# Self-attention block on one core: another set of planner parameters, and the output projection of the third query block in one piece

## The chip, the core and the metric

The kernel runs on one core of one Trainium2 chip. The metric is the device time of one execution in microseconds. A core has five engines that run side by side and wait for each other through semaphores: TensorE (PE in the profile, its weight loads PEld), VectorE (DVE), ScalarE (ACT), GpSimd (POOL) and SyncE (SP, which here only issues transfers).

## The reference

Inputs: x of 1x2048x448, wqkv of 448x1344, wo of 448x448, all in bfloat16. Sixteen heads of width 28.

```python
qkv = transpose((x @ wqkv).reshape(B, S, 3, H, Dh), 2, 0, 3, 1, 4)
scores = einsum("bhqd,bhkd->bhqk", q, k) * (Dh ** -0.5)
p = softmax(scores, axis=-1)
o = einsum("bhqk,bhkd->bhqd", p, v)
return transpose(o, 0, 2, 1, 3).reshape(B, S, D) @ wo
```

The exponentials, 16 x 2048 x 2048 of them, are most of the work that is not a matmul.

## The kernel before

The sixteen heads are four groups g of four heads; the queries are four blocks c of 512. One (g, c) is a window, 16 in all, run g by g. A window has 16 rows of keys (128 keys each) times four heads, so 64 tiles of 128x512 scores, 1024 tiles in all; `WT` is 64 and `NT` 1024.

Per tile, `emit_S` (L656) computes the transposed scores into PSUM. Two engines make exponentials of them:

- ScalarE (L946) takes two tiles at once from a double bank PA_199 or PA_200 and writes a PTA tile of 128x1024.
- VectorE and GpSimd share another tile, from a single bank PD_201, PD_202 or PD_203, in `start_tile` (L744): the first pass on VectorE (L751) scales the low 16 bits of the scores to DU, the second pass on VectorE (L754) multiplies the same low halves from PSUM with DU and makes DV, GpSimd (L757) multiplies DV by DU and makes DG, and the third pass on VectorE (L770) adds DG to the scores and writes the bits of a bfloat16 into a PTD tile. The product is a cubic correction of the exponential's mantissa.

A row of four exponentials then goes through four small matmuls with the values (`pv_op`, L807), which sum into bank PO; a column of ones in the values gives the denominators. At the end of a window `finish_window` copies PO to OSB (L698), sends the denominators through DRAM to all partitions (L723 to L728, issued by SyncE), and GpSimd multiplies (L731) into OT[g][c]. Once all four groups of a block c are there, `task_OP(c)` (L613) multiplies them by wo: four blocks of 128 queries, for each a sum over g of matmuls of 128x448, then a copy by VectorE, then the block's store (L635). Block 3, the last window's, is done by code behind the plan (L1062 on): the last two rows of keys are left over (`NLAST`), `task_pre` (L590) sums three groups of the projection ahead, `partial_sums` copies PO (L688) and gathers the denominators by matmul into PD_203 (L674), and then L1080 to L1102 add the last two rows, normalise, project and store.

The order of every engine's instructions is not written out: a planner in the kernel (L991 on) simulates the engines with assumed durations (`P1`, `PTT`, `MM` and others), picks for each engine the ready task of the lowest priority number, and then emits the instructions in the order found. On the chip each engine runs its list in that order. The parameters that the change touches steer it:

- `O1`, `O2`, `OF`: tile n's first, second and third pass have the priorities n - O1, n - O2 and n - OF.
- `NTAIL`: VectorE takes no tiles within the last NTAIL; from there the single banks are free for the tasks of the end.
- `GLAT`: the time the planner assumes for the broadcast of the denominators (L728).
- `J0`, `J3`, `JL`: how many rows must be ready before a window's first PV; J3 is for the last four windows except the very last, which has JL.
- `SLK`: by how much a task on TensorE may run past the end of an exponential when the next scores are due.
- `DI`: with how many VectorE tiles under way, at least, the projection may be taken early near the end.

With `SPLIT = (2,)` block 2's projection is cut in two: `task_part` (L600) sums groups 0 to 2 (L605) during the last four windows, where PARTD, PARTE and PARTU set its priority, its earliest moment and the point from which it may use any single bank, and VectorE copies the sums in float32 (L608) into the space of a key tile no longer used. `task_OP` then does group 3 alone for that block (L621), and VectorE adds the stored sums (L625) in place of the copy (L628).

Of the kernel before, what the change touches and what calls it, by code (L numbers as in the profile page):

```python
# [10 lines left out]
ALU = mybir.AluOpType  # L11
# [3 lines left out]
F32 = mybir.dt.float32  # L15
# [3 lines left out]
P = 128  # L19
H = 16  # L20
HP = 32
G = 4
# [17 lines left out]
SEM = 0.13  # L40
# [35 lines left out]
def kernel(  # L76
# [7 lines left out]
    nc = tc.nc  # L84
    _, S, D = x.shape
# [4 lines left out]
    TPC = QW // P  # L90
# [13 lines left out]
    PMODE = 'g'  # L104
    PBACK = 3
    J0 = 9
    NTAIL = 12
    JL = 6
    DI = 2
    WPE = 1  # L110
    PVM = 0.0
    ADUR = 0.25
# [6 lines left out]
    PFIN = 0.3  # L119
    QEA = 30  # L120
    PLT = 6.0
    GLAT = 6.5
    J3 = 9
    UQ = 16
    OD = 4
    PADQ = 1
    O1 = 30
    O2 = 10
    OF = 0.4
    RV = 2  # L130
    QPR = 100
    LOOK = 0.2
    SLK = 0.13
    MG = 0.1
    SPLIT = (2,)
    PARTD = 60
    PARTE = -4
    PARTU = 40
    UO = 40

    x2 = x[0]
# [15 lines left out]
    WO = sb([P, G, D], BF16, "WO")  # L157
# [4 lines left out]
    KB = [[sb([P, S], BF16, f"KB{b}_{pr}") for pr in range(2)] for b in range(2)]  # L162
# [4 lines left out]
    OT = [[sb([P, QW], BF16, f"OT{g}_{c}") for c in range(NQC)] for g in range(G)]  # L167
# [11 lines left out]
    OUTS = XS  # L179
# [62 lines left out]
    for i in range(HG):  # L242
        nc.sync.dma_start(out=WO[HP * i:HP * i + Dh, :, :],
                          in_=bass.AP(wo.tensor, wo.offset + i * Dh * D, [[D, Dh], [HG * Dh * D, G], [1, D]]))
# [3 lines left out]
    NT = G * NQC * NKT * HG  # L248
# [8 lines left out]
    def add(op):  # L257
        static[op.eng].append(op)
        return op

    def bank_task():
        return {"slot": None}

    def acq_d(task, early=False, urgent=1e9):
        def f(t):
            if task["slot"] is not None:
                return True
            free = [s for s in ([o_slot] + d_slots if early or pos[0] >= min(urgent, NT - NTAIL) else [o_slot]) if s.free_at <= t + 1e-9]
            if not free:
                return False  # L270
            s = free[-1]
            s.free_at = 1e18
            task["slot"] = s
            return True
        return f
# [4 lines left out]
    def at(n):  # L280
        return lambda t: pos[0] >= n

    def bank(task):
        return (PD + [PO])[task["slot"].idx]
# [76 lines left out]
    WT = NKT * HG  # L361

    def chain_mm(n, fn, deps, prio, elig, acq):
        ops = []
        for k in range(n):
            o = add(Op("PE", MM, (lambda k=k: fn(k)), deps=deps if k == 0 else [ops[-1]], prio=prio + 0.001 * k, kind="B",
                       elig=elig, acq=acq if k == 0 else None, lat=0.0 if k < n - 1 else PLAT))
            ops.append(o)
        return ops
# [205 lines left out]
    ot_done = {}  # L575
# [16 lines left out]
                [ot_done[(g, c)] for g in range(G - 1)], NT + 900 + tq * 10, None, hold(acq, tq))  # L592

    op_left = [TPC * (NQC - 1)]
    parts = {}

    def part(c, tq):
        return KB[0][tq // 2][:].bitcast(F32)[:, (tq % 2) * D:(tq % 2 + 1) * D]

    def task_part(c):  # L600
        due = (12 + c) * WT - PARTD
        for tq in range(TPC):
            task = bank_task()
            ap = (lambda task=task: bank(task)[:, 0:D])
            ops = chain_mm(G - 1, lambda g, tq=tq, ap=ap: nc.tensor.matmul(  # L605
                out=ap(), lhsT=OT[g][c][:, tq * P:(tq + 1) * P], rhs=WO[:, g, :], start=(g == 0), stop=(g == G - 2)),
                [ot_done[(g, c)] for g in range(G - 1)], due + tq * 10, at(12 * WT - PARTE), acq_d(task, urgent=due + PARTU))
            ev = add(Op("DVE", 0.54, lambda tq=tq, ap=ap: nc.vector.tensor_copy(out=part(c, tq), in_=ap()),  # L608
                        deps=[ops[-1]], prio=due - 1000))
            ev.after = lambda t, task=task: setattr(task["slot"], "free_at", t + SEM)  # L610
            parts[(c, tq)] = ev

    def task_OP(c):  # L613
        due = (12 + c + 1) * WT + 16
        st = add(Op("SP", 0.05, None, prio=due))
        evs = []
        for tq in range(TPC):
            task = bank_task()
            ap = (lambda task=task: bank(task)[:, 0:D])
            g0 = G - 1 if c in SPLIT else 0  # L620
            ops = chain_mm(G - g0, lambda k, tq=tq, ap=ap: nc.tensor.matmul(  # L621
                out=ap(), lhsT=OT[g0 + k][c][:, tq * P:(tq + 1) * P], rhs=WO[:, g0 + k, :], start=(k == 0), stop=(g0 + k == G - 1)),
                [ot_done[(g, c)] for g in range(g0, G)], due + tq * 10, None, acq_d(task, urgent=NT - UO))
            if g0:
                ev = add(Op("DVE", 0.56, lambda tq=tq, ap=ap: nc.vector.tensor_tensor(  # L625
                    out=OUTS[c][:, tq, :], in0=ap(), in1=part(c, tq), op=ALU.add), deps=[ops[-1], parts[(c, tq)]], prio=due - 1000))
            else:
                ev = add(Op("DVE", 0.54, lambda tq=tq, ap=ap: nc.vector.tensor_copy(out=OUTS[c][:, tq, :], in_=ap()),  # L628
                            deps=[ops[-1]], prio=due - 1000))
            def aft(t, task=task):  # L630
                op_left[0] -= 1
                task["slot"].free_at = t + SEM
            ev.after = aft
            evs.append(ev)
        add(Op("SP", 0.05, lambda: nc.sync.dma_start(out=out_perm[:, c * TPC:(c + 1) * TPC, :], in_=OUTS[c][:]),  # L635
               deps=evs, prio=due))
# [55 lines left out]
    def finish_window(w, t):  # L692
        g, c = divmod(w, NQC)
        b = norm_n[0] % 2
        norm_n[0] += 1
        pvop = rows[(w, NKT - 1)]["pv"]
        prev = norm_busy[b]
        ev = add(Op("DVE", 0.62, lambda: nc.vector.tensor_copy(out=OSB[b][:], in_=PO[:]), deps=[pvop] + ([prev] if prev else []),  # L698
                    prio=-5000))

        def rel(t):
            o_slot.free_at = t + SEM
        ev.after = rel

        if w >= NW - WPE:
            ev.after = None
            d1 = chain_A(lambda tq: den_gather(PO, lambda k: OSB[b][:, k * P:(k + 1) * P], (tq,)), [ev])
            d2 = add(Op("DVE", 0.17, lambda: nc.vector.reciprocal(out=RT[:], in_=PO[:, 0:TPC * HG]), deps=[d1], prio=-5000))
            d2a = [add(Op("DVE", 0.25, lambda hf=hf: den_expand(hf, nc.vector.tensor_copy), deps=[d2], prio=-5000)) for hf in range(2)]
            d2b = chain_A(lambda tq: den_spread(PO, (tq,)), d2a)  # L710
            d3 = add(Op("DVE", 0.62, lambda: nc.vector.tensor_tensor(out=OT[g][c][:], in0=OSB[b][:], in1=PO[:], op=ALU.mult),
                        deps=[d2b], prio=-5000))
            d3.after = rel
            norm_busy[b] = d3
            ot_done[(g, c)] = d3
            if (g, c) == (G - 2, NQC - 1):
                task_pre()
            if g == G - 2 and c in SPLIT:
                task_part(c)
            if g == G - 1:  # L720
                task_OP(c)
            return
        o1 = [add(Op("SP", 0.6, lambda: nc.sync.dma_start(  # L723
            out=DCO[b][:], in_=OSB[b][Dh::HP, :].rearrange("i (a b) -> i a b", b=TPC * HG)), deps=[ev], prio=-10, lat=2.6))]
        o2 = add(Op("DVE", 0.17, lambda: nc.vector.reciprocal(out=DRC[b][:], in_=DCO[b][:]), deps=o1, prio=-4000))
        o3 = add(Op("SP", 0.4, lambda: nc.sync.dma_start(out=SCR[b][:].rearrange("i (a b) -> (i a) b", b=TPC * HG),
                                                         in_=DRC[b][:]), deps=[o2], prio=-10, lat=2.0))
        o4 = [add(Op("SP", 0.6, lambda: nc.sync.dma_start(  # L728
            out=RRB[b][:], in_=bass.AP(SCR[b][:].tensor, SCR[b][:].offset, [[QW, HG], [0, HP], [1, QW]])),
            deps=[o3], prio=-10, lat=GLAT))]  # L730
        o5 = add(Op("POOL", 1.22, lambda: nc.gpsimd.tensor_tensor(out=OT[g][c][:], in0=OSB[b][:], in1=RRB[b][:], op=ALU.mult),  # L731
                    deps=o4, prio=-10, kind="n"))
        norm_busy[b] = o5
        ot_done[(g, c)] = o5
        if (g, c) == (G - 2, NQC - 1):
            task_pre()
        if g == G - 2 and c in SPLIT:
            task_part(c)
        if g == G - 1:
            task_OP(c)  # L740

# [249 lines left out]
    while True:  # L991
        if not times:
            break
        t = heapq.heappop(times)
# [67 lines left out]
    c = NQC - 1  # L1062
    g = G - 1
# [11 lines left out]
    for j in range(NKT - NLAST, NKT):  # L1075
        pt = rows[(NW - 1, j)]["p"]
        for i in range(HG):
            for tq in range(TPC):
                col = tq * HG + SI[i]
                nc.tensor.matmul(out=PD[2][:, col:col + 1], lhsT=pt[i][1]()[:, tq * P:(tq + 1) * P],  # L1080
                                 rhs=VA[g][:, 0, 0, Dh:Dh + 1], start=False, stop=(j == NKT - 1), skip_group_check=True)
        for i in range(HG):
            st = SI[i]
            nc.tensor.matmul(out=PO[HP * st:HP * (st + 1), :], lhsT=VA[g][:, j, st, :], rhs=pt[i][1](),
                             start=False, stop=(j == NKT - 1), tile_position=(0, HP * st), skip_group_check=True)
# [44 lines left out]
```

## Time and profile before

| what | value |
|---|---|
| three runs | 416.57, 416.38, 416.83 us; median 416.57 |
| profiled execution | 416.57 us, of which the span from first to last instruction is 414.5 |
| busy: TensorE | 364.7 us (88% of the span) |
| busy: VectorE | 396.0 us (96%), 700 instructions |
| busy: ScalarE | 399.6 us (96%), 439 instructions |
| busy: GpSimd | 226.3 us (55%), 211 instructions |
| chain that ended last | ScalarE 85%, issue 7%, TensorE 5% |
| granted TensorE clock | 1.000 |
| transfers | 15.85 MB, 14.4% of 16 engines' span on the main queue |

An engine that waits inside an instruction's queue shows as idle time in front of it, with the releaser's name. ScalarE's and VectorE's instructions overlap a little in the record: a VectorE pass lasts 0.68 us, but follows the one before by 0.60, and the exponential of two tiles is recorded with 0.92 to 1.29 us while they follow each other every 0.917. Where a chain of such instructions is counted, the distance from start to start is the cost. The chain of waits goes back from the last instruction and names what each one waited for.

### The profile page before, as it was taken

Reading aid. Unit: us, or ns where it says so; the run is one execution under the profiler, and the core shown is the slowest. Engines: PE = TensorE matmul, PEld = TensorE weight load, DVE = VectorE, ACT = ScalarE, POOL = GpSimd, SP = SyncE. Lnnn points to the kernel's source line nnn. Section 1 sums busy time; section 2 is a strip of 40 time slices with the busy share of each in tenths; the row PEclk is TensorE's granted clock in tenths of the full one; section 3 lists DMA queues with packets and bytes.
Section 4 is the critical chain, followed back from the end, with each engine's and each line's share of the span. In section 5 each row is a group of like instructions: output and inputs, shape, how many; then the busy total and the mean of one; then the engine's idle time right before and its main releaser. Section 6 shows DMA issues by size and latency. Waiting matters only on the chain.

```text
span 414.5 us, 7646 instructions
## 1 busy us (share of the span) xinstructions
PE 364.7 (88%) x2655; PEld 124.8 (30%) x2668; DVE 396.0 (96%) x700; ACT 399.6 (96%) x439; POOL 226.3 (55%) x211
## 2 busy tenths in 40 slices
PE   8988989898988889898897988889897988989996
PEld 5433222323232232323222222222322222222324
DVE  6899999999999999999999999999999999999983
ACT  4999999999999999999999999999999999999992
POOL 3155456474656656475555646456474656556450
PEclk9999999999999999999999999999999999999999
DMA  8410010202201002111400001010410101001012
GB/s 258 76 19 21 3 49 9 55 22 56 69 2 46 0 22 36 26 32 23 100 3 29 18 19 30 2 41 6 90 35 12 36 1 47 0 27 47 20 53 90
DMA packets 33414, 15.85 MB, mean 38 GB/s; under 512 B 26016, under 2 KB 30304, under 8 KB 33376
## 3 DMA queue, kind: packets, MB, share of 16 engines
q1 hardware_dynamic: 32304, 15.05, 14.4%
q8 instruction: 21, 0.34, 0.3%
q10 hardware_dynamic: 1072, 0.32, 0.3%
q14 instruction: 17, 0.14, 0.1%
HBM read 7.37 MB, written 1.96 MB: 23 GB/s over the span
## 4 chain that ended last, share of the span: by engine, by line
ACT 85%; issue 7%; PE 5%; DMA 1%; DVE 1%; SPq 0%; DVEq 0%
ACT PTA_132 L946 4%; ACT PTA_133 L946 4%; ACT PTA_131 L946 4%; ACT PTA_134 L946 4%; ACT PTA_140 L946 4%; ACT PTA_139 L946 4%; ACT PTA_138 L946 4%; ACT PTA_137 L946 4%; ACT PTA_136 L946 4%; ACT PTA_135 L946 4%; ACT PTA_145 L946 4%; ACT PTA_141 L946 4%; ACT PTA_144 L946 3%; ACT PTA_148 L946 3%; ACT PTA_149 L946 3%
## 5 line engine op out<-in xcount | busy, mean ns | idle before, releaser
L757 POOL TENSOR_TENSOR DG_183<-DV_177,DU_171 128x512 f16<-128x512 f16 x30 | 34.7, 1155 | 36.9 <-DVE DV_177 L754 36.7
L757 POOL TENSOR_TENSOR DG_184<-DV_178,DU_172 128x512 f16<-128x512 f16 x30 | 34.7, 1156 | 30.1 <-DVE DV_178 L754 29.5
L757 POOL TENSOR_TENSOR DG_186<-DV_180,DU_174 128x512 f16<-128x512 f16 x29 | 33.5, 1155 | 30.7 <-DVE DV_180 L754 29.3
L757 POOL TENSOR_TENSOR DG_185<-DV_179,DU_173 128x512 f16<-128x512 f16 x30 | 34.7, 1156 | 23.6 <-DVE DV_179 L754 23.5
L757 POOL TENSOR_TENSOR DG_188<-DV_182,DU_176 128x512 f16<-128x512 f16 x29 | 33.5, 1155 | 24.1 <-DVE DV_182 L754 23.0
L757 POOL TENSOR_TENSOR DG_187<-DV_181,DU_175 128x512 f16<-128x512 f16 x29 | 33.5, 1156 | 23.6 <-DVE DV_181 L754 23.4
L656 PEld LDWEIGHTS <-KB_1_94 64*128 64x128 bf16 x256 | 20.5, 93 | 46.1 <-issue 45.1
L656 PEld LDWEIGHTS <-KB_0_93 64*128 64x128 bf16 x256 | 20.5, 93 | 46.0 <-issue 45.0
L656 PEld LDWEIGHTS <-KB_0_91 64*128 64x128 bf16 x256 | 20.4, 92 | 45.0 <-issue 41.3
L656 PEld LDWEIGHTS <-KB_1_92 64*128 64x128 bf16 x256 | 20.1, 92 | 45.3 <-issue 43.4
L946 ACT ACTIVATE PTA_145<-PA_199 128x1024 bf16<-128x1024 f32 x18 | 22.5, 1253 | 0.0
L946 ACT ACTIVATE PTA_144<-PA_200 128x1024 bf16<-128x1024 f32 x18 | 22.5, 1247 | 0.0
L946 ACT ACTIVATE PTA_140<-PA_200 128x1024 bf16<-128x1024 f32 x18 | 22.4, 1247 | 0.0
L946 ACT ACTIVATE PTA_143<-PA_199 128x1024 bf16<-128x1024 f32 x18 | 22.4, 1244 | 0.0
L946 ACT ACTIVATE PTA_142<-PA_200 128x1024 bf16<-128x1024 f32 x18 | 22.3, 1240 | 0.0
L946 ACT ACTIVATE PTA_141<-PA_199 128x1024 bf16<-128x1024 f32 x18 | 22.3, 1237 | 0.0
L946 ACT ACTIVATE PTA_146<-PA_200 128x1024 bf16<-128x1024 f32 (+1 forms) x18 | 21.9, 1216 | 0.0
L946 ACT ACTIVATE PTA_139<-PA_199 128x1024 bf16<-128x1024 f32 x17 | 21.1, 1242 | 0.0
L946 ACT ACTIVATE PTA_147<-PA_199 128x1024 bf16<-128x1024 f32 x17 | 21.1, 1241 | 0.0
L751 DVE TENSOR_SCALAR DU_173<-PD_203 128x512 f16<-128x512 uint16 x29 | 19.8, 682 | 0.9 <-PE PD_203 L656 0.7
L751 DVE TENSOR_SCALAR DU_171<-PD_201 128x512 f16<-128x512 uint16 x29 | 19.8, 681 | 0.9 <-PE PD_201 L656 0.9
L751 DVE TENSOR_SCALAR DU_174<-PD_201 128x512 f16<-128x512 uint16 x29 | 19.7, 680 | 0.7 <-PE PD_201 L656 0.7
(632 smaller groups left out, 1516.6 us busy)
## 6 DMA issues: line engine op xcount, KB each, us to landing
RRB_195<-SCR_197 SPq DMA_DIRECT2D x8, 256.0 KB
RRB_196<-SCR_198 SPq DMA_DIRECT2D x7, 256.0 KB
KB_1_94<-KB_0_93 SPq DMA_DIRECT2D x4, 128.0 KB
XS_127<-in_x_dram SPq DMA_DIRECT2D x1, 448.0 KB
XS_128<-in_x_dram SPq DMA_DIRECT2D x1, 448.0 KB
XS_129<-in_x_dram SPq DMA_DIRECT2D x1, 448.0 KB
XS_130<-in_x_dram SPq DMA_DIRECT2D x1, 448.0 KB
out_dram<-XS_127 SPq DMA_DIRECT2D x1, 448.0 KB
```

The costliest lines, as they stand in the source:

```text
L656: nc.tensor.matmul(out=ap, lhsT=KB[g % 2][i // 2][a:a + 64, j * P:(j + 1) * P], rhs=QB[w % NQB][i // 2][a:a + 64, :], start=True, stop=Tru ...
L751: p1 = add(Op("DVE", P1, lambda: nc.vector.tensor_scalar(out=DU[b][:], in0=lo, scalar1=SIG / 65536, scalar2=SIG * (SS - 0.5), op0=ALU.mult ...
L757: gq = add(Op("POOL", PTT, lambda: nc.gpsimd.tensor_tensor(out=DG[b][:], in0=DV[b][:], in1=DU[b][:], op=ALU.mult), deps=[p2], prio=n, kind ...
L946: nc.scalar.activation(out=PTA[pslot.idx][:, 0:len(ns) * QW], in_=PA[s.idx][:, 0:len(ns) * QW], func=ACT.Exp, bias=ACT_BIAS, scale=ACT_SCALE)
```

## The change

Described in a few words, the change is: "VectorE's tile: second pass multiplies the scores' low halves from PSUM with the first pass's result, GpSimd makes the cubic's last product for every tile, in place of: VectorE tiles free of the share". The diff has two parts. It sets eight planner parameters to other values, and it takes out SPLIT with all that belongs to it, so that block 2's projection is one sum over four groups, as those of blocks 0 and 1 are. The lines of VectorE's tile (L751 to L773) are the same in both kernels.

```diff
-    NTAIL = 12
+    NTAIL = 6
     JL = 6
-    DI = 2
+    DI = 1
...
-    GLAT = 6.5
-    J3 = 9
+    GLAT = 7.0
+    J3 = 7
     UQ = 16
     OD = 4
     PADQ = 1
-    O1 = 30
-    O2 = 10
-    OF = 0.4
+    O1 = 20
+    O2 = 20
+    OF = 10
     RV = 2
     QPR = 100
     LOOK = 0.2
-    SLK = 0.13
+    SLK = 0.15
     MG = 0.1
-    SPLIT = (2,)
-    PARTD = 60
-    PARTE = -4
-    PARTU = 40
     UO = 40
...
-    parts = {}
-
-    def part(c, tq):
-        return KB[0][tq // 2][:].bitcast(F32)[:, (tq % 2) * D:(tq % 2 + 1) * D]
-
-    def task_part(c):
...
     def task_OP(c):
...
-            g0 = G - 1 if c in SPLIT else 0
-            ops = chain_mm(G - g0, lambda k, tq=tq, ap=ap: nc.tensor.matmul(
-                out=ap(), lhsT=OT[g0 + k][c][:, tq * P:(tq + 1) * P], rhs=WO[:, g0 + k, :], start=(k == 0), stop=(g0 + k == G - 1)),
-                [ot_done[(g, c)] for g in range(g0, G)], due + tq * 10, None, acq_d(task, urgent=NT - UO))
-            if g0:
-                ev = add(Op("DVE", 0.56, lambda tq=tq, ap=ap: nc.vector.tensor_tensor(
-                    out=OUTS[c][:, tq, :], in0=ap(), in1=part(c, tq), op=ALU.add), deps=[ops[-1], parts[(c, tq)]], prio=due - 1000))
-            else:
-                ev = add(Op("DVE", 0.54, lambda tq=tq, ap=ap: nc.vector.tensor_copy(out=OUTS[c][:, tq, :], in_=ap()),
-                            deps=[ops[-1]], prio=due - 1000))
+            ops = chain_mm(G, lambda g, tq=tq, ap=ap: nc.tensor.matmul(
+                out=ap(), lhsT=OT[g][c][:, tq * P:(tq + 1) * P], rhs=WO[:, g, :], start=(g == 0), stop=(g == G - 1)),
+                [ot_done[(g, c)] for g in range(G)], due + tq * 10, None, acq_d(task, urgent=NT - UO))
+            ev = add(Op("DVE", 0.54, lambda tq=tq, ap=ap: nc.vector.tensor_copy(out=OUTS[c][:, tq, :], in_=ap()),
+                        deps=[ops[-1]], prio=due - 1000))
...
-            if g == G - 2 and c in SPLIT:
-                task_part(c)
```

The last two lines are taken out at both places where `finish_window` had them.

More of the change, by code (lines that the diff above doesn't have):

```diff
@@ L594 @@
     op_left = [TPC * (NQC - 1)]
-    parts = {}
-    def part(c, tq):
-        return KB[0][tq // 2][:].bitcast(F32)[:, (tq % 2) * D:(tq % 2 + 1) * D]
-    def task_part(c):
[L601 to L608, printed above, removed]
-                        deps=[ops[-1]], prio=due - 1000))
-            ev.after = lambda t, task=task: setattr(task["slot"], "free_at", t + SEM)
-            parts[(c, tq)] = ev
     def task_OP(c):
@@ L619, in task_OP @@
             ap = (lambda task=task: bank(task)[:, 0:D])
-            g0 = G - 1 if c in SPLIT else 0
-            ops = chain_mm(G - g0, lambda k, tq=tq, ap=ap: nc.tensor.matmul(
-                out=ap(), lhsT=OT[g0 + k][c][:, tq * P:(tq + 1) * P], rhs=WO[:, g0 + k, :], start=(k == 0), stop=(g0 + k == G - 1)),
-                [ot_done[(g, c)] for g in range(g0, G)], due + tq * 10, None, acq_d(task, urgent=NT - UO))
-            if g0:
-                ev = add(Op("DVE", 0.56, lambda tq=tq, ap=ap: nc.vector.tensor_tensor(
-                    out=OUTS[c][:, tq, :], in0=ap(), in1=part(c, tq), op=ALU.add), deps=[ops[-1], parts[(c, tq)]], prio=due - 1000))
-            else:
-                ev = add(Op("DVE", 0.54, lambda tq=tq, ap=ap: nc.vector.tensor_copy(out=OUTS[c][:, tq, :], in_=ap()),
-                            deps=[ops[-1]], prio=due - 1000))
+            ops = chain_mm(G, lambda g, tq=tq, ap=ap: nc.tensor.matmul(
[3 more added lines that the diff above has]
+                        deps=[ops[-1]], prio=due - 1000))
             def aft(t, task=task):
@@ L736, in finish_window @@
             task_pre()
-        if g == G - 2 and c in SPLIT:
-            task_part(c)
         if g == G - 1:
```

## The prediction

> **What bounds the kernel now.** I read the page's busy shares, then the table by stage, then the chain that ended last, then the timeline of the last 14 us. ScalarE (96%) and VectorE (96%) tie on the page, so the stages decide. Two rows of that table (columns: stretch, length, busy us of PE, PEld, DVE, ACT, POOL, clock, DMA share, GB/s):
>
> ```profile
> 20.00:400.00 380.00, 336.32 (x2417) 109.17 (x2428) 373.94 (x644) 380.00 (x416) 220.14 (x191) 1.00 0.12 30
> 404.46:414.60 10.14, 6.19 (x71) 4.17 (x69) 3.74 (x9) 1.96 (x4) 0.00 (x0) 1.00 0.26 92
> ```
>
> From 20 to 400 us ScalarE has no idle time at all (380.00 of 380.00), VectorE has 6 us, TensorE 44. The exponentials end one after another: the first ends at 16.19 + 1.02 = 17.21, the last whole one (two tiles) at 403.17 + 1.29 = 404.46, so 422 steps take 387.25 us, 0.918 each; the undisturbed run at 18.47 to 36.80 us has 0.917. At most 422 x 0.001 = 0.5 us is lost in the whole stretch. After 404.46 ScalarE has nothing to do, and the chain goes over to TensorE:
>
> ```profile
> 403.61 0.35 PE PA_200 L656
> 403.96 0.30 PE PD_203 L621
> 404.26 0.57 PE PD_201 L590 x3
> 404.83 0.38 PE PD_202 L590 x2
> 405.21 0.82 PE PD_203 L674 x8
> 406.03 0.21 PE PD_202 L590
> 406.24 0.38 PE PD_203 L1080 x16
> ```
>
> So the end is a sum: 424 passes of ScalarE, then what TensorE has queued behind the last score matmul (403.59), in its fixed order. Between that matmul and the first L1080 (406.08 in the timeline) lie one output projection matmul, six of the last block's, and the gather of the denominators. From 406.08 on (last two rows of keys, normalisation, last projection, stores) 8.4 us of span follow, the same instructions in both kernels.
>
> **The change, part by part.**
>
> The words promise a new form of VectorE's tile. The diff has no line of it: the second pass on low halves (L754) and GpSimd's product (L757, 177 tiles) already stand in the kernel before. That part costs nothing.
>
> The exponentials. The built order gives ScalarE 424 passes in both kernels; before, the last one holds one tile, now two (847 and 848 tiles; VectorE's tiles fall from 177 to 176). The last pass starts after 423 others either way, at 404.09; it ends later by half a step, 0.917 - 0.49 = 0.43 us, at about 405.4. TensorE reads it last, after 409 by the walk below, so this is hidden; without cover it would cost 0.43.
>
> The split projection that goes (block 2, parameters SPLIT, PARTD, PARTE, PARTU). Before, twelve of its sixteen matmuls (L605) and four copies (L608) ran at 314 to 326 us, between score matmuls:
>
> ```profile
> 318.67 0.36 PE L605 MATMUL PO<-WO,OT_2_113 128*128 128x448 bf16 x1
> 318.87 0.35 PE L605 MATMUL PO<-WO,OT_2_117 128*128 128x448 bf16 x1
> 320.07 0.62 DVE L608 COPY KB_1_92<-PO 128x448 f32<-128x448 f32 x1
> ```
>
> They cost TensorE 12 x 0.19 = 2.3 us (0.19 from start to start) and VectorE 4 x 0.61 = 2.4 us, but in a stretch where ScalarE never waited. Taking them away frees nothing on the path: 0. VectorE also loses one tile, 3 x 0.60 = 1.8 us, and the four adds become copies (0.62 against 0.61). About 4 us of VectorE work go. VectorE is not last anywhere in 20 to 400 us, so this is worth 0, and up to 0.5 us (all that ScalarE lost there).
>
> [...]
>
> Where those matmuls come back. Block 2's projection is now sixteen matmuls (four blocks of 128 rows, four groups each) in one sum, and the fourth group's operand, OT_2_125, is only made by GpSimd at 398.93 to 400.2. The code lets the first of a sum wait for all four, so all sixteen stand behind it; before, twelve had been done in the middle. By the built order, five stand before the last score pair (two after the fourth last pair, two after the third last, one after the second last), eleven after it; before, three of four stood ahead and one behind. Also twelve PV matmuls (three rows of keys) now stand behind the last pair; before, none did. I walk TensorE's queue, with starts from the timeline:
>
> ```profile
> 403.59 0.37 PE L656 MATMUL PA_200<-QB_1_86,KB_1_94 64*128 64x512 bf16 x1
> 404.30 0.62 DVE L625 TENSOR_TENSOR XS_129<-PD_203,KB_1_92 128x448 bf16<-128x448 f32 x1
> 404.97 0.97 PEld L674 LDWEIGHTS PD_203<-sel,OSB_190 128*128 128x128 f32 x8 [0.21 <-DVE XS_129 L625]
> 405.89 0.35 PE L590 MATMUL PD_202<-WO,OT_3_122 128*128 128x448 bf16 x1
> ```
>
> - 403.59: last pair; both halves start together as other pairs do (402.68). Its bank comes free with the exponential that ends at 403.54, as before.
> - 403.91: one projection matmul (score to projection is 403.59 to 403.90).
> - 404.21: three rows of PV, 0.22 each (403.00 and 403.23 before), so to 404.65; PV to the next kind 0.33.
> - 404.98: ten projection matmuls at 0.19, to 406.88. Then one of L590, to 407.07.
> - Gather (L674): it needs the last rows' copy OSB_190 and bank PD_203 copied out. VectorE: OSB_190 starts 0.43 after the last PV (403.24 to 403.67), 405.08; the copies of PD_202 at 405.68 and of PD_203 at 406.33 (its last matmul at 405.93 plus 0.40, from 403.90 to 404.30); that ends at 406.95. TensorE arrives at 407.07: no wait.
> - 0.92 for the gather (404.97 to 405.89): 407.99. Five more of L590, 0.95: first L1080 at 408.94. The last copy (PD_201) ends at 407.7, before its bank is needed.
>
> 408.94 against 406.08 is **+2.86 us**. As a check by count: ten more projection matmuls 1.9, three PV rows 0.66, two changes of kind about 0.2 to 0.3: 2.8 to 2.9.
>
> The planner's numbers (NTAIL, DI, GLAT, J3, O1, O2, OF, SLK). They only reorder. TensorE: between neighbouring score pairs the built order holds the same mix as before (eight PV matmuls 84 times, 82 before; no gap that holds more than the fullest before), so no pair must come late. VectorE: first and second pass now stand next to each other 42 times, 33 before; a neighbour costs 0.12 (301.00 to 301.72 against 0.60), 1 us of the 4 saved. GpSimd's product takes 2.0 us from the start of the second pass (301.72 to 302.55, and 1.16 for itself). The third pass stands three places behind the second or further in both orders; three places are 1.8 us, so 0.2 of waiting, 8 times now against 3 before, 1 us more of the 4. The tiles of VectorE are used 6 or more score pairs after their own matmul, as before; one exception, the very last tile, has 4 (below). GLAT moves GpSimd's normalisation of a block behind one more product at most; its row ended at 400.2, and the matmul that reads it stands behind the third last score pair, at 402.3. No row shows what a new order does to ScalarE; the ends are 0.5 us below nothing (what was lost) and 2 us above (0.12, a near neighbour's cost, in each of 16 windows). I take 0, the nearest row being 380.00 of 380.00 under the same mix. The store of block 2 (L635) is issued after the last copy, at 407.8 in place of 404.95; the queue moved its bytes by 407.1, so 2.2 us, and it is through by 410, before the first final store (410.68 plus 2.9). Nothing, with 3 us to spare.
>
> **Sum.** The profiled execution took 416.57 us, its span 414.5; it is also the median of the runs. 416.57 + 2.86 = 419.4.
>
> **Rivals.**
>
> 1. *ScalarE waits in the middle.* The third pass is planned earlier (OF 10), so VectorE may stand waiting for GpSimd, with the first passes of other tiles queued behind it, then PV rows and, in TensorE's order, the next pair. For: VectorE has 6 idle us in 380. Against: the distances above. Price 0.5 to 2 us over the forecast: 420 to 421.5. I give 0.17.
> 2. *The tail is shorter.* If a part of the eleven overlaps a wait that I do not see, or the pairs end earlier, half of the 2.86 is left: 418.0. Against: before, TensorE's only gap there was 0.21 us, so there is little to overlap with. 0.08.
> 3. *Faster: VectorE sets the pace.* If the 96% VectorE and not ScalarE is what holds the score banks, 4.2 us less work there (2.4 and 1.8) gives up to 4.2, less the 2.86 of the tail: 415.2. It decides from more than 2.9 us of real ScalarE waits; the rows show 0.5. 0.03.
> 4. *The change does not do what its words say,* and the rest cancels: no tile changes, and the walk of the tail is wrong by the whole sum: 416.6. 0.03.
>
> A variant of 1: the last tile. Its score matmul is at 400.2; first pass 400.5, second 401.2, GpSimd 402.0, third pass at 403.3 behind a copy, ready at 403.9; PV wants it at 404.65. If VectorE is 0.8 us late, each further 0.1 is paid in full. It is part of the 0.17.
>
> **Chances.** Forecast 0.69, rivals 0.17, 0.08, 0.03, 0.03. A run of this kernel can tell about 0.2% (0.8 us) from no change. Faster 0.03; within 0.2%: 0.04; slower 0.93. The forecast's own range is 418.9 (0.5 that ScalarE had lost) to 419.8 (four switches of kind in the walk at 0.1 each). With rival 2 (418.0) and rival 1 up to 421.0 the range 418.0 to 421.0 holds some 0.88; without rival 2 or the upper half of rival 1 it would fall to 0.8 or below.
>
> **What would show it.** Right: ScalarE again 380.00 of 380 between 20 and 400 us; its last exponential starts near 404.1 and is two tiles wide; eleven projection matmuls and three PV rows after the last pair; first L1080 (its line moves) near 408.9; from there 8.4 us. Wrong: idle ScalarE in the middle, a gather that waits on VectorE, or a last pair that is not at 403.6.

## The result, and the profile after

The changed kernel takes 419.11 us (median of 4 runs, 418.80 to 419.26), the kernel before beside it 416.54. The ratio is 1.006, with a 95% interval of 1.0042 to 1.0077: 2.6 us slower. The forecast was 419.4, the range 418.0 to 421.0. The profiled execution took 419.18 us, its span is 417.4 (before 414.5).

The same two rows of the table by stage, after (stretch, length, busy us of PE, PEld, DVE, ACT, POOL, clock, DMA share, GB/s; the second stretch is longer because the span is):

```profile
20.00:400.00 380.00, 332.94 (x2402) 108.86 (x2414) 371.10 (x634) 380.00 (x416) 216.59 (x189) 1.00 0.12 30
404.46:417.50 13.04, 9.12 (x94) 5.48 (x90) 5.73 (x12) 2.50 (x5) 0.00 (x0) 0.94 0.20 72
```

ScalarE is again busy in 380.00 of 380.00 us. Its first exponential ends 0.15 us later than before (17.36), its last whole one before the final pass 0.11 later (404.57): over 422 steps nothing is won or lost. VectorE has 2.8 us less to do in that stretch, TensorE 3.4, and it buys nothing. All the rest lies behind 404.46, where TensorE is busy for 9.1 us in place of 6.2. The chain that ended last, from the last pair of score matmuls (L630; before L656) to the first matmul of the last two rows (L1050; before L1080):

```profile
403.81 0.32 PE PA_200 L630 x2
404.13 0.29 PE PD_202 L599
404.43 0.76 PE PO L777 x12
405.19 0.48 PE PD_202 L599 x2
405.67 0.76 PE PD_203 L599 x4
406.43 0.76 PE PD_201 L599 x4
407.19 0.19 PE PD_202 L586
407.37 0.83 PE PD_203 L648 x8
408.20 0.59 PE PD_201 L586 x3
408.79 0.38 PE PD_202 L586 x2
409.17 0.38 PE PD_203 L1050 x16
```

These are the eleven projection matmuls (L599), the three PV rows (L777 x12), the six of block 3 (L586) and the gather (L648) of the walk, in its order. In the timeline the last pair starts at 403.74 and the first L1050 at 409.00, 5.26 us; before it was 403.59 to 406.08, 2.49 us. So the queue behind the last pair grew by 2.77 us, and it starts 0.15 later.

### The profile page after: what moved, and what is told of

Same layout as the page of the kernel before. It is cut to its first block, busy times and chain, and to the rows that moved or that the text cites. A ratio compares the mean times of both kernels' runs of the same rounds, so it can differ in the third digit from the quotient of the medians.

```text
span 417.4 us, 7639 instructions
## 1 busy us (share of the span) xinstructions
PE 364.9 (87%) x2660; PEld 126.2 (30%) x2673; DVE 395.2 (95%) x693; ACT 399.9 (96%) x439; POOL 224.3 (54%) x210
## 4 chain that ended last, share of the span: by engine, by line
ACT 77%; PE 11%; issue 6%; DVE 3%; DMA 2%; SPq 0%; DVEq 0%
ACT PTA_133 L916 4%; ACT PTA_132 L916 4%; ACT PTA_131 L916 4%; ACT PTA_135 L916 4%; ACT PTA_134 L916 4%; ACT PTA_136 L916 3%; ACT PTA_150 L916 3%; ACT PTA_145 L916 3%; ACT PTA_138 L916 3%; ACT PTA_144 L916 3%; ACT PTA_137 L916 3%; ACT PTA_140 L916 3%; ACT PTA_146 L916 3%; ACT PTA_148 L916 3%; ACT PTA_143 L916 3%
## 5 line engine op out<-in xcount | busy, mean ns | idle before, releaser
L630 PEld LDWEIGHTS <-KB_1_94 64*128 64x128 bf16 x256 | 21.3, 92 | 51.8 <-issue 50.6
L630 PEld LDWEIGHTS <-KB_0_91 64*128 64x128 bf16 x256 | 19.9, 92 | 45.9 <-issue 42.4
L630 PEld LDWEIGHTS <-KB_1_92 64*128 64x128 bf16 x256 | 20.2, 93 | 43.0 <-issue 41.0
L630 PEld LDWEIGHTS <-KB_0_93 64*128 64x128 bf16 x256 | 19.5, 93 | 43.3 <-issue 42.5
L916 ACT ACTIVATE PTA_144<-PA_200 128x1024 bf16<-128x1024 f32 x18 | 22.3, 1239 | 0.0
L916 ACT ACTIVATE PTA_143<-PA_199 128x1024 bf16<-128x1024 f32 x18 | 22.2, 1235 | 0.0
L916 ACT ACTIVATE PTA_142<-PA_200 128x1024 bf16<-128x1024 f32 x18 | 22.2, 1233 | 0.0
L721 DVE TENSOR_SCALAR DU_174<-PD_201 128x512 f16<-128x512 uint16 x29 | 19.7, 681 | 1.6 <-PE PD_201 L630 1.3
L916 ACT ACTIVATE PTA_141<-PA_199 128x1024 bf16<-128x1024 f32 x17 | 21.1, 1240 | 0.0
L916 ACT ACTIVATE PTA_145<-PA_199 128x1024 bf16<-128x1024 f32 x17 | 21.1, 1239 | 0.0
L721 DVE TENSOR_SCALAR DU_172<-PD_202 128x512 f16<-128x512 uint16 x29 | 19.8, 683 | 0.8 <-PE PD_203 L630 0.5
L721 DVE TENSOR_SCALAR DU_175<-PD_202 128x512 f16<-128x512 uint16 x28 | 19.1, 684 | 1.5 <-PE PD_202 L630 1.5
L721 DVE TENSOR_SCALAR DU_173<-PD_203 128x512 f16<-128x512 uint16 x29 | 19.8, 682 | 0.3 <-PE PD_203 L630 0.2
L724 DVE SCALAR_TENSOR_TENSOR DV_177<-PD_201,DU_171 128x512 f16<-128x512 uint16 x29 | 19.8, 682 | 0.2
L721 DVE TENSOR_SCALAR DU_171<-PD_201 128x512 f16<-128x512 uint16 x29 | 19.8, 682 | 0.3 <-PE PD_201 L630 0.2
L724 DVE SCALAR_TENSOR_TENSOR DV_180<-PD_201,DU_174 128x512 f16<-128x512 uint16 x29 | 19.8, 682 | 0.2
```

The source lines that it names most:

```text
L630: nc.tensor.matmul(out=ap, lhsT=KB[g % 2][i // 2][a:a + 64, j * P:(j + 1) * P], rhs=QB[w % NQB][i // 2][a:a + 64, :], start=True, stop=Tru ...
L721: p1 = add(Op("DVE", P1, lambda: nc.vector.tensor_scalar(out=DU[b][:], in0=lo, scalar1=SIG / 65536, scalar2=SIG * (SS - 0.5), op0=ALU.mult ...
L724: p2 = add(Op("DVE", P1, lambda: nc.vector.scalar_tensor_tensor(out=DV[b][:], in0=lo, scalar=65536 * (SS - 0.5 + CE / C3), in1=DU[b][:], o ...
L916: nc.scalar.activation(out=PTA[pslot.idx][:, 0:len(ns) * QW], in_=PA[s.idx][:, 0:len(ns) * QW], func=ACT.Exp, bias=ACT_BIAS, scale=ACT_SCALE)
```

## The experiments

Theory: the time is ScalarE's passes, 0.917 us each, plus the queue behind the last score pair. Rivals: the planner's numbers alone or the split alone carry the loss; VectorE sets the pace in the middle; VectorE, not TensorE, sets the queue at the end. "Before" is the median of the kernel before on the same chip; the ratio is taken over the single runs and need not be exactly that of the two medians.

| run | us, median (lowest to highest) | before | ratio, 95% interval |
|---|---|---|---|
| e1, split kept, new numbers | 419.17 (418.85 to 419.36) | 416.56 | 1.0061, 1.0049 to 1.0073 |
| e2, no split, old numbers | 418.69 (418.47 to 418.98) | 416.56 | 1.0051, 1.0039 to 1.0063 |
| e4, middle's matmuls and copies out | 418.63 (417.76 to 419.73) | 416.56 | 1.0049, 1.0037 to 1.0061 |
| e5, six matmuls of the end out | 419.18 (418.67 to 419.21) | 416.56 | 1.0057, 1.0044 to 1.0070 |
| e6, only the middle's copies out | 416.66 (416.42 to 417.00) | 416.75 | 1.0000, 0.9991 to 1.0008 |
| e7, eight matmuls and two copies of the end out | 418.79 (418.51 to 421.62) | 416.75 | 1.0050, 1.0037 to 1.0064 |
| e8, O2 alone | 420.47 (420.41 to 420.88) | 416.69 | 1.0092, 1.0079 to 1.0105 |
| e9, last block early, J0 = 10 | 417.24 (415.99 to 417.70) | 416.69 | 1.0005, 0.9995 to 1.0015 |
| e10, the same, J0 = 8 and RV = 3 | 418.73 (416.74 to 419.75) | 416.69 | 1.0045, 1.0031 to 1.0058 |
| e11, the same, J3 = 10 and UO = 50 | 417.73 (416.14 to 418.38) | 416.69 | 1.0015, 1.0004 to 1.0026 |
| e12, zeros in the middle | 416.54 (416.42 to 417.07) | 416.52 | 1.0002, 0.9993 to 1.0012 |
| e13, e10 once more | 419.85 (one run) | 416.52 | |

### One half of the change at a time (e1, e2)

e1 is the kernel before with the eight new numbers; e2 is the kernel before with `SPLIT = ()`.

> The kernel before with the eight new planner numbers, the split kept. The built order has 425 passes of ScalarE (the last with one tile, 849 in all, against 847 before), and behind the last score matmul three output projection matmuls more and three PV rows (12 matmuls) more than before. Theory (the time is ScalarE's passes, plus the queue behind the last score matmul): 0.92 for one more pass, 0.19 x 2 for projection and 0.66 plus changes of kind for the PV rows, about 2.3 us over before: 418.9. Rival (the split projection alone carries the loss): 416.5. Second rival (the numbers cost by idle time of ScalarE in the middle): 418 to 419 too, but with ScalarE below 380.00 of 380 between 20 and 400 us.

> The kernel before without the split, its planner numbers kept. Behind the last score matmul 13 projection matmuls of block 2 in place of one, no PV row more, 424 passes of one tile in the last. Theory: 12 x 0.19 = 2.3 us over before: 418.8. Rival (the new numbers alone carry the loss): 416.5. Rival (VectorE sets the pace in the middle, and gains from the four copies that go): 1 us or more below 418.8.

e2 is 2.1 us slower, 12 x 0.19 = 2.3 to within 0.2. The chain of e2 from its last score matmul on:

```profile
404.07 0.35 PE PA L656
404.42 2.56 PE PD L621 x13
406.98 0.95 PE PD L590 x5
407.93 0.83 PE PD L674 x8
408.76 0.21 PE PD L590
408.96 0.38 PE PD L1080 x16
```

Here TensorE runs from the last pair to the end without a pause; against before only the thirteen projection matmuls in place of one differ. In the timeline the stretch from the last score matmul to the first L1080 is 404.05 to 408.80, 2.26 us longer than before; in this execution the first exponential also ended 0.44 later (17.65).

e1 is 2.6 us slower, with ScalarE at 380.00 of 380. It has a pass more (425): its last score matmul stands at 404.36, 0.77 later than before, although its first exponential ends 0.23 earlier (16.98). From there to the first L1080 (408.88) it takes 4.52 us, 2.03 more than before, where the expectation counted 1.04 plus changes of kind. The chain shows what the count left out, a stretch on VectorE:

```profile
404.47 0.62 DVE XS L625
405.09 0.59 DVE PTD L770
405.69 1.07 DVE XS L625 x2
406.76 0.04 issue
406.81 0.73 PE PD L590 x3
```

An add of the projection, the third pass of a late tile and two more adds come one after the other, and the matmuls of block 3 (L590) wait 0.29 us for the last of them. So either half costs about as much as both together. Neither rival that gives the loss to one half alone stands, and the two are not a sum: the numbers make the planner divide the tiles between the engines anew, and what the end costs depends on the order that comes out.

### What the middle is worth (e4, e6, e12)

In e4 the twelve matmuls of L605 and the four copies of L608 are not issued, all else keeps its place. In e6 only the copies are left out, in e12 the copies are left out as in e4, but matmuls of zeros stand in for the twelve.

```diff
-            ops = chain_mm(G - 1, lambda g, tq=tq, ap=ap: nc.tensor.matmul(
-                out=ap(), lhsT=OT[g][c][:, tq * P:(tq + 1) * P], rhs=WO[:, g, :], start=(g == 0), stop=(g == G - 2)),
+            ops = chain_mm(G - 1, lambda g: None,
...
-            ev = add(Op("DVE", 0.54, lambda tq=tq, ap=ap: nc.vector.tensor_copy(out=part(c, tq), in_=ap()),
+            ev = add(Op("DVE", 0.54, None,
```

> The kernel before with the same plan, but the twelve partial projection matmuls (L605) and the four copies (L608) at 314 to 326 us are not issued; block 2's output then lacks groups 0 to 2. Theory: they lay beside a ScalarE that never waited, so nothing changes: 416.5, within 0.3. Rival (VectorE sets the pace): 2.4 us less, 414.1.

> The kernel before with the same plan, the twelve partial matmuls (L605) kept, only the four copies (L608) not issued, so that block 2's output lacks groups 0 to 2. It differs from the run that left out both by the matmuls alone. Theory (VectorE's work in the middle is free, and the earlier run lost its 2 us because TensorE, with less to do there, was granted half its clock): 416.5, with the clock at 1.00 from 312 to 332 us. Rival (VectorE sets the pace): 414.1. Rival (the missing copies themselves upset the order, by letting others start at another time): about 418.6, with or without the clock.

> As the run that left out the middle's partial matmuls and copies, but twelve matmuls of zeros with the same shape stand in the place of the twelve partial ones; block 2's output lacks groups 0 to 2. Theory (the 2 us lost there came from TensorE's clock, which fell because its queue was thinned, whatever the matmuls compute): back at 416.6, clock 1.00 from 312 to 332 us. Rival (it is the data or the order of waits that counted): 418 or more.

e4 missed on both sides: less work, and 2.1 us more time. The table by stage of e4, for 312 to 332 us and for the worst part of it:

```profile
312.00:332.00 20.00, 15.23 (x77) 2.85 (x73) 16.36 (x28) 18.55 (x21) 10.26 (x9) 0.74 0.08 24
317.00:324.00 7.00, 6.06 (x21) 1.04 (x21) 5.06 (x8) 6.62 (x8) 3.60 (x4) 0.51 0.11 38
```

The number behind the five busy times is the clock that TensorE was granted: 0.51 of full speed from 317 to 324 us, and ScalarE, which never waits before, loses 1.45 of the 20 us. The last pair of e4 stands at 405.39, 1.8 us later than before, and from there to the first matmul of the last rows it takes 2.49 us, as before: all of the loss lies ahead of the end. The mean granted clock is 0.980 to 0.987 in all six executions of e4, and 0.998 to 1.000 in those of the kernel before. The same 20 us of e6 and then of e12:

```profile
312.00:332.00 20.00, 17.01 (x105) 5.05 (x104) 18.26 (x31) 20.00 (x24) 11.65 (x10) 1.00 0.09 25
```

```profile
312.00:332.00 20.00, 17.14 (x106) 5.12 (x106) 18.27 (x32) 20.00 (x23) 11.60 (x10) 1.00 0.08 25
```

With the matmuls back, real ones or zeros, the clock is 1.00 and the time is that of before. So 2.4 us of VectorE's work in the middle are worth nothing, as forecast, and the rival by which VectorE sets the pace falls. TensorE's 2.3 us there are worth nothing as work either (with them ScalarE is busy in 20.00 of the 20 us), but the granted clock of these 20 us is 1.00 with them (e6, e12) and 0.74 without (e4). The kernel's planner has an assumption of its own on this: it keeps a sum of what its simulated TensorE did lately (`WINDOW`, L54), and where the sum falls below a bound (`BAR`, L55) and TensorE has time and a bank for it, it puts in a matmul of zeros (L907). No run here tests that window or that bound. In e4 the planner did not know that the twelve matmuls would be missing.

### What holds the end (e5, e7)

e5 and e7 are the changed kernel with its order kept; in e5 the sums of the last two quarters of block 2 are cut to group 3, in e7 those sums and their two copies go altogether.

```diff
-            ops = chain_mm(G, lambda g, tq=tq, ap=ap: nc.tensor.matmul(
-                out=ap(), lhsT=OT[g][c][:, tq * P:(tq + 1) * P], rhs=WO[:, g, :], start=(g == 0), stop=(g == G - 1)),
+            g0 = G - 1 if c == 2 and tq > 1 else 0
+            ops = chain_mm(G, lambda g, tq=tq, ap=ap, g0=g0: None if g < g0 else nc.tensor.matmul(
+                out=ap(), lhsT=OT[g][c][:, tq * P:(tq + 1) * P], rhs=WO[:, g, :], start=(g == g0), stop=(g == G - 1)),
```

> The changed kernel with the same plan, but for the last two quarters of block 2 (the sums in PD_203 and the second in PD_201) only group 3's matmul is issued, so six of the eleven projection matmuls behind the last pair go; that half of block 2's output then lacks groups 0 to 2. Forecast's step (TensorE's queue alone sets the gather): 6 x 0.19 = 1.1 us less, 418.0. Rival (VectorE's three copies in a row, of PO, PD_202 and PD_203, hold the gather at about the same moment, as the 0.21 us of wait in the trace after suggests): within 0.2 of the changed kernel, 419.0.

> The changed kernel with the same plan, without the eight projection matmuls of the last two quarters of block 2 and without their two copies, so that half of block 2's output is missing. If TensorE's queue alone sets the end: 8 x 0.19 = 1.5 us less, 417.6. If VectorE's row of copies ties with it: the copy of PD_202 is still needed (its bank is used next), it ends at 406.5 in the trace after; then one matmul and the gather at about 406.7 in place of 407.2: 0.5 us less, 418.6.

e5 takes as long as the changed kernel, although 1.1 us of TensorE's work are gone. Its chain shows what took their place:

```profile
404.52 0.82 PE PO L778 x12
405.34 0.02 issue
405.36 0.69 DVE OSB L663
406.05 1.07 DVE XS L603 x2
407.13 0.04 issue
407.17 1.05 PE PD L649 x8
```

From the last PV row the path goes over VectorE: the copy of PO, then the copies of PD_202 and PD_203 (the bank of the gather), one after the other, until 407.13; the gather starts at 407.17, as in the changed kernel (407.14). There the same row of VectorE stands beside TensorE's; the timeline of the changed kernel has it:

```profile
405.26 0.69 DVE L662 COPY OSB_190<-PO 128x512 f32<-128x512 f32 x1 [1.15 <-PE PO L777]
405.87 0.61 DVE L602 CAST XS_129<-PD_202 128x448 bf16<-128x448 f32 x1
406.47 0.62 DVE L602 CAST XS_129<-PD_203 128x448 bf16<-128x448 f32 x1
407.14 0.97 PEld L648 LDWEIGHTS PD_203<-sel,OSB_190 128*128 128x128 f32 x8 [0.21 <-DVE XS_129 L602]
407.21 0.99 PE L648 MATMUL PD_203<-sel,OSB_190 128*128 128x4 f32 x8
```

The copy of PD_203 ends at 407.09 (406.47 + 0.62). TensorE's queue, with the matmul ahead at 407.02 and 0.19 from start to start, reaches the gather at 407.21. The two paths end within some 0.1 us of each other, and to shorten TensorE's alone gains next to nothing: from the last pair to the first matmul of the last rows e5 takes 5.19 us (403.84 to 409.03), the changed kernel 5.26. In e7, where one copy less stands in front of the gather, five of the seven runs lie at 418.51 to 419.03, their median 418.76. That is 2.01 us over the kernel before on the same chip, and the changed kernel is 2.57 over it on its own, so 0.56 less; the row of copies called for 0.5 and TensorE's queue for 1.5. (The other two take 421.23 and 421.62, with a mean clock of 0.988 against 0.998 to 1.000 in the five. The first of them was profiled: from 145 to 155 us the clock was granted at 0.50 to 0.56, and ScalarE lost 2.1 us, in an order that the changed kernel has too, where the clock is 1.00 in that stretch.) In the chain of the profiled one 4.83 us lie between the last pair and the first matmul of the last rows, against 5.36 in the changed kernel's chain: 0.53 less.

### Passes against tail (e8)

```diff
-    O2 = 10
+    O2 = 20
```

> The kernel before with one number changed, O2 = 20 for 10 (the second pass planned earlier), the split kept. The built order has 427 passes of ScalarE in place of 424 (VectorE takes 170 tiles in place of 177) and two projection matmuls more behind the last pair. Theory (passes of ScalarE plus the queue behind the last pair): 3 x 0.917 + 2 x 0.19 = 3.1 us over before, 419.7. Rival (only what stands behind the last pair counts, VectorE's tiles are made up elsewhere): 417.0. Rival (VectorE sets the pace, so seven tiles less are a gain): below 416.

3.8 us over before, 0.7 more than the theory, and against both rivals. The passes are as priced: the last pair stands at 406.54, 2.95 after 403.59, of which 0.18 is a later first exponential (17.39) and 2.77 the three passes. What was missed is VectorE again. From the last PV row of e8 on:

```profile
406.36 0.69 DVE OSB L688
407.05 1.07 DVE XS L625 x2
408.13 0.04 issue
408.17 1.29 PE PD L590 x6
409.46 0.82 PE PD L674 x8
```

The six matmuls of block 3 need banks that VectorE copies out only after PO, so they wait until 408.17 and then stand in line with the gather: 3.61 us from last pair to first L1080 (410.15 in the timeline), where the count of matmuls gave 2.9.

### A version that shortens the end (e9, e10, e11, e13)

If the end is TensorE's queue, block 3's early sums (L590) can go the way of block 2's: summed in the middle, kept in bfloat16, added by VectorE in the last copies. The gather moves to PD_202, whose copy is done earlier. e9, e10 and e11 differ in planner numbers alone; `RV` is how many rows must be ready for PV to go ahead of other tasks, and `UO` sets from which tile on the projection may take any single bank.

```diff
-            ops = chain_mm(G - 1, lambda g, tq=tq: nc.tensor.matmul(
-                out=PD[tq][:, 0:D], lhsT=OT[g][c][:, tq * P:(tq + 1) * P], rhs=WO[:, g, :], start=(g == 0), stop=False),
-                [ot_done[(g, c)] for g in range(G - 1)], NT + 900 + tq * 10, None, hold(acq, tq))
+            ops = chain_mm(G - 1, lambda g, tq=tq, ap=ap: nc.tensor.matmul(
+                out=ap(), lhsT=OT[g][c][:, tq * P:(tq + 1) * P], rhs=WO[:, g, :], start=(g == 0), stop=(g == G - 2)),
+                [ot_done[(g, c)] for g in range(G - 1)], due + tq * 10, at(12 * WT + 4), acq_d(task, urgent=due + PARTU))
+            ev = add(Op("DVE", 0.54, lambda tq=tq, ap=ap: nc.vector.tensor_copy(out=PART3[tq][:], in_=ap()),
+                        deps=[ops[-1]], prio=due - 1000))
...
-        (nc.scalar.copy if tq % 2 == 0 else nc.vector.tensor_copy)(out=OUTF[tq][:], in_=fb[tq])
+        if tq < 2:
+            nc.vector.tensor_tensor(out=OUTF[tq][:], in0=fb[tq], in1=PART3[tq][:], op=ALU.add)
+        else:
+            nc.scalar.copy(out=OUTF[tq][:], in_=fb[tq])
```

> A version of the kernel before, meant to be faster: two quarters of block 3's projection (groups 0 to 2) are summed in the middle, as block 2's are, and kept in bfloat16; VectorE adds them in the two last copies; ScalarE copies the other two quarters; the gather goes to PD_202, so it need not wait for the copy of PD_203; J0 = 10. The built order has 424 passes, and one projection matmul and the gather behind the last pair. Theory: the gather at 404.1 and the first matmul of the last two rows at 405.05 in place of 406.08, the rest unchanged: 1.0 us less, 415.5. Rival (VectorE's copies hold the gather or the end): 416.3 to 416.8.

> The same edit with J0 = 8 and RV = 3 in place of J0 = 10: eight PV matmuls stand between the last two pairs, 424 passes, one projection matmul and the gather behind the last pair. Theory: as the run before, but the copy of PO starts later, at about 403.9, so the gather waits for it until 404.6: 0.6 us less, 416.0. Rival (a clock that falls in the middle because fewer matmuls fill it): 417 or more.

> The same edit with J3 = 10 and UO = 50 in place of J0 = 10: two projection matmuls and the gather behind the last pair, 424 passes. Theory: 0.2 us more than with J0 = 10, 415.7. Rival: as there.

> The version with J0 = 8 and RV = 3 once more, for its profile alone: its runs lay at 416.7 to 419.8, and the profile was of the fastest. Theory (a clock that falls in some executions): where this one is above 418, a stretch with a granted clock near 0.50 and idle time of ScalarE in it; where it is near 416.7, none. Rival (VectorE late by the new order): idle time of ScalarE at clock 1.00.

Only the best executions come near the expectation: 415.99 in e9, 0.7 below before and 0.5 above its forecast, with the gather waiting for VectorE until 404.53. The medians are no better than before (e9) or worse (e10, e11), and the single runs of one kernel lie 1.7 to 3.0 us apart. e13 is the program of e10 once more, in an execution of 419.85 us. Its end, by stage:

```profile
404.00:406.00 2.00, 1.28 (x13) 0.48 (x6) 1.70 (x3) 2.00 (x3) 0.00 (x0) 1.00 0.00 0
406.00:408.00 2.00, 2.00 (x37) 1.55 (x37) 0.00 (x0) 0.14 (x1) 0.00 (x0) 0.66 0.57 229
408.00:410.00 2.00, 2.00 (x21) 1.07 (x19) 1.28 (x4) 0.40 (x1) 0.00 (x0) 0.50 0.03 8
```

The clock falls to half just where the last matmuls run, and stays there until 412 (0.50 from 410 to 412 too); in the profiled execution of e10 (416.74 us) it was 1.00 from 406 to 410. Of the 3.1 us between the two, 2.8 lie behind the start of the gather (405.76 to the last cast at 414.49, against 405.13 to 411.09). The loss is thus not, as expected, idle time of ScalarE in the middle, of which there is 0.23 us, at 270 to 276 us. TensorE waits 0.72 us for VectorE in front of the gather in both executions, in time that the matmuls taken out of the end had filled; so the wait alone does not decide whether the clock falls. That the clock makes the time is shown for this one execution: four matmuls of the end (L1100) take 0.85 us in its chain, from 410.12 at a clock of 0.50, and 0.45 us in that of e10, from 408.40 at 1.00. For the spread of e9, e10 and e11 it is inferred, from the mean clock of each execution: it is 0.997 to 1.000 in the 12 of up to 416.82 us, and 0.990 to 0.996 in the 23 of 417.24 us or more. No version here beats the kernel before in its median.

## Why the prediction was right

**ScalarE bounds the middle.** Right: 380.00 of 380.00 after, and e6 shows that VectorE's copies are worth nothing there. Rival 3 (VectorE sets the pace) is out, rival 1 did not occur.

**The split's matmuls and copies in the middle cost nothing.** Right as to the work; the reason given, a stretch where ScalarE never waits, was only half the story, since without the matmuls the clock fell (0.51 from 317 to 324 us in e4) and ScalarE did wait (busy in 18.55 of the 20 us). The prediction did not weigh the clock. In the changed kernel the planner puts in more matmuls of zeros (57 weight loads of zeros at L877, 52 at L907 before), and the clock is 1.00 from 20 to 400 us and in every 2 us from 402 to 414, past TensorE's last matmul (413.58; the 0.94 in the table by stage comes from the time after, 0.72 from 415 us on); that these very ones keep it up was not tried.

**The walk of the end, +2.86.** Measured: 2.92 at the first L1050, of which 0.15 came from the start of the kernel and 2.77 from the queue. The parts agree: the copy of PO at 405.26 (walk 405.08), the gather at 407.14 to 407.21 (walk 407.07), the copy of PD_203 at 406.47 (walk 406.33), first L1050 at 409.00 (walk 408.94). Span plus 2.9. The profiled execution grew by 2.61 and the median by 2.57, since the time around the span fell from 2.07 to 1.78; that 0.3 is why the forecast is 0.3 too high.

**The step that was only half right** is the check by count, in which ten matmuls at 0.19 cost 1.9 us. "TensorE arrives at 407.07: no wait" nearly holds: the 0.21 us beside the gather is idle time of the weight loads (before has the same), and from the gather's first matmul to the next matmul it is 0.85 us, against 0.80 in e7, where no copy held it. But the walk's own numbers put VectorE's copies only 0.12 us ahead of TensorE (406.95 against 407.07), and measured it is 0.12 again (407.09 against 407.21). That margin is all that TensorE's queue can lose before the copies hold the gather, and e5 shows it: six of those matmuls go for nothing. The sum came out because TensorE's path was walked rightly and VectorE's ends just ahead of it; as a statement of what the matmuls cost, 0.19 each, the check was wrong for this order. It is right in e2, where the four copies start 0.75 us apart (404.75 to 407.02), in step with the sums of four matmuls, and TensorE sets the pace.

**The planner's numbers at 0.** Not tested as such by the sum: e1 shows that by themselves they cost 2.6 us, through a pass more, other work behind the last pair, and a stretch on VectorE there. In the changed kernel the order built had 424 passes, and that, read off beforehand, is what made the 0 right. Rival 4 (all cancels) is out; the words of the change indeed move nothing, as no line of VectorE's tile differs. That both halves together cost no more than either alone was not forecast and is not explained beyond the order that came out. Rival 2 (a shorter end) is out by the measured 5.26 us.

## What to carry to other kernels

Where one engine is saturated and another finishes the kernel, as here, the time is the passes of the first plus what stands behind the last hand-over. Work moved out of the first stretch into the second can be paid in full (e2: 2.1 us for twelve matmuls), and work of another engine removed from the first stretch was worth nothing (e6: 2.4 us of VectorE, 416.66 us against 416.75). Walk the second with every engine that copies out a bank, since two paths that tie hide each other, and a count of one engine's instructions then misleads (e5: 1.1 us of matmuls out, 419.18 us against 419.11). Before thinning a queue of matmuls, look at the granted clock of that stretch: here it was 1.00 with twelve of them (e6, e12), and 0.51 from 317 to 324 us without (e4).

## What had not been expected of the hardware

In e4 TensorE's granted clock fell to half without a long pause ahead of it. From 313.7 to 317.4 us TensorE issued a pair of score matmuls every 0.92 us and one single, with no wait above 0.53 us, and from 317.4 the matmuls last 0.61 us in place of 0.39; the clock is 1.00 from 312 to 316 us and 0.50 from 318 to 322. With the twelve matmuls over 12 us (e6), or with twelve of zeros (e12), it is 1.00 from 312 to 332 us. Two pairs of e4, before and after the fall:

```profile
314.61 0.39 PE L655 MATMUL PA<-QB,KB 64*128 64x512 bf16 x2 [0.53 <-ACT PTA L945]
317.36 0.61 PE L655 MATMUL PA<-QB,KB 64*128 64x512 bf16 x2 [0.33 <-ACT PTA L945]
```

Leaving out 2.3 us of matmuls cost 2.1 us (418.63 against 416.56). What decides the fall is not shown. In e4 waits of 0.33 to 0.53 us, repeated, stand ahead of it; in e10 and e13 one wait of 0.72 us in front of the gather is followed by a clock of 1.00 from 406 to 410 us in the first, and of 0.50 from 408 to 412 in the second.
